# Loading K and V units in runs of 1 KB instead of 4 KB per partition

## The chip, the cores and the metric

The kernel runs on one core of one Trainium2 chip. The metric is the device time of one execution in microseconds. Every kernel was executed several times, and the tables give medians. The kernel before was run again beside each group of experiments, on the same chip. Its median was 697.37 us beside the change, and 700.1, 701.38 and 696.53 us beside the three groups of experiments. One of its runs beside the first group was marked as slow and is left out of the ratios.

## The reference

It is a decode step with two attention layers and two feed-forward layers that share their weights and their K and V caches:

```python
B, Sq, D = 4, 1, 512
Hq, Hkv, Sk, Dh = 32, 8, 8192, 128        # k_cache, v_cache: (B, Hkv, Sk, Dh), bf16, 67 MB each
...
scores = jnp.einsum("bhqd,bhkd->bhqk", q, k) * (Dh ** -0.5)
p = _softmax(scores, axis=-1)
o = jnp.einsum("bhqk,bhkd->bhqd", p, v)
...
x = x + _A_ref(_layernorm(x, axis=-1), A_k_cache, A_v_cache, A_wq, A_wo)   # attention
x = x + _B_ref(_layernorm(x, axis=-1), B_w_gate, B_w_up, B_w_down)         # feed-forward
x = x + _A_ref(...)                                                        # the same once more
x = x + _B_ref(...)
```

The softmax and the sum over keys do not depend on the order of the keys, as long as K and V are permuted alike.

## The kernel before

The caches are read in units of 2,048 rows of one head, 512 KB each. A unit goes into a slot with 4 KB in each of the 128 partitions. There are 7 ring slots, and 11 kept slots that hold some V units for the second layer. In all 468 units are loaded (256 of K, and 168 + 44 of V), all from the queue of the SP engine, in a fixed order. Each partition receives 16 neighbouring rows, one run of 4 KB:

```python
CR = 2048; NB = CR // P; NRING = 7; NRET = 11
ring = sb("ring", [P, NRING, NB * Dh], BF16)
kept = sb("kept", [P, NRET, NB * Dh], BF16)
# ... cut ...
def pump():                                  # issues loads in order while their slots are free
    while lptr[0] < len(loads):
        kind, x, sm = loads[lptr[0]]
        if kind == "w":
            T.dma("sp", x[0], x[1], sm, writes=[x[2]])       # a weight piece
        else:
            ap, key = home[x]
            if not released.get(key, True):
                return
            released[key] = False
            _, l, b, g, c = x
            cache = A_k_cache if x[0] == "k" else A_v_cache
            src = cache[b, g, c * CR:(c + 1) * CR, :].rearrange("(p t) d -> p (t d)", p=P)
            T.dma("sp", ap, src, sm, writes=[key])
        lptr[0] += 1
```

A K unit is transposed block by block on TensorE (16 transposes), copied out of PSUM by VectorE or ScalarE, and multiplied with q (4 matmuls). A V unit is the stationary operand of 16 matmuls with 4 columns:

```python
for t in range(8):                           # in k_front, for each half of a K unit
    blk = hf * 8 + t
    T.op("pe", lambda e: e.matmul(stg[:, t * P:(t + 1) * P], lhsT=ap[:, blk * Dh:(blk + 1) * Dh],
                                  rhs=ident[:], is_transpose=True, start=True, stop=True), ...)
# ... cut: in v_unit, for m in range(NM), j in range(NJ) ...
T.op("pe", lambda e: e.matmul(ps[:, bk * BW:bk * BW + REP],
                              lhsT=ap[:, (NM * j + m) * Dh:(NM * j + m + 1) * Dh],
                              rhs=pp[:, q, col:col + REP], ...), ...)
```

Between the streams of units lie stretches in which TensorE works on projections, feed-forward layers and softmax, and on kept V units that need no load in the second layer.

## Time and profile before

| | before |
|---|---|
| median time | 697.37 us |
| span of the profiled run | 699.7 us |
| TensorE (PE) busy | 584.9 us, 84% |
| share of the DMA engines in queue 1 | 96.1% |
| unit of 512 KB, from issue to landing | 7.6 us |

From the page of the profile of the kernel before (PE is TensorE, PEld its weight loads, DVE VectorE, ACT ScalarE; SPq is the SP engine's issuing queue): span and busy time; then, over 40 equal slices of the span, the granted TensorE clock in tenths, the busy share of the 16 DMA engines in tenths, and the GB/s that they moved; the packets by size; the queue of the loads with packets, MB and share of the engines; the chain of work that ended last; and the two costliest groups with "busy, mean ns of one | idle time before them, and what ended most of it".

```profile
span 699.7 us, 25539 instructions
...
PE 584.9 (84%) x11552; PEld 479.2 (68%) x11552; DVE 298.8 (43%) x635; ACT 235.1 (34%) x296; POOL 0.7 (0%) x6
...
PEclk9999879995589889985599879995589955599855
DMA  8999999999889999999999999999899989999992
GB/s 349 388 388 408 385 395 407 401 401 409 328 284 411 404 399 407 406 408 392 335 343 409 402 370 385 370 409 407 320 382 409 408 325 410 349 338 361 343 396 75
DMA packets 75117, 260.93 MB, mean 373 GB/s; under 512 B 7672, under 2 KB 13568, under 8 KB 74496
...
q1 hardware_dynamic: 75008, 259.30, 96.1%
...
PE 51%; DMA 37%; issue 5%; DVE 4%; ACT 2%; SPq 1%; ACTq 0%
DMA ring<-in_A_k_cache_dram 27%; PE ps L408 25%; PE ps L507 9%; DMA ring<-in_A_v_cache_dram 8%; PE ps L424 7%; PE ps L572 3%; PE ps L596 2%; DMA wq_sb<-in_A_wq_dram 2%; PE ps L531 1%; SPq L92 1%; PE ps L632 1%; PE ps L548 1%; ACT ktp L248 1%; PE ps L479 1%; DVE negm L436 1%
...
L408 PE MATMUL ps<-ident,ring 128*128 128x128 bf16 x4096 | 294.6, 230 | 36.8 <-DMA ring<-in_A_k_cache_dram 35.0
L408 PEld LDWEIGHTS ps<-ident,ring 128*128 128x128 bf16 x4096 | 251.4, 103 | 79.0 <-DMA ring<-in_A_k_cache_dram 54.1
...
ring<-in_A_k_cache_dram SPq DMA_DIRECT2D x256, 512.0 KB, 7.6
```

The reader should see three things here. The DMA engines are busy nearly throughout, at 385 to 411 GB/s in most slices. In some slices (328, 284, 335, 343, 320, 325 and so on) they move much less: there, TensorE is in a stretch that frees no ring slot. And the groups of TensorE on line 408, the K transposes, wait mostly for ring loads of K. The chain, with 37% DMA and 51% PE, passes between the two.

### The profile page before, as it was taken

What the parts mean: (1) busy time and instruction counts of PE and PEld (TensorE: products, weight loads), DVE (VectorE), ACT (ScalarE), POOL (GpSimd) and SP (SyncE); (2) the same over time, 40 slices, a digit from 0 to 9 for tenths busy, and PEclk for the clock granted to TensorE, in tenths of its full rate; (3) what the DMA queues carried; (4) which work ended last, traced back from release to release, by engine and by line L of the source; (5) the groups of instructions that cost most, each with busy time, mean ns of one, the idle gap of its engine ahead of it and who ended that gap; (6) DMA issues with size and microseconds to landing.
All of it is one profiled execution on the core that took longest, in us unless ns stands there. A gap on an engine that the chain in (4) does not pass through costs nothing.

```text
span 699.7 us, 25539 instructions
## 1 busy us (share of the span) xinstructions
PE 584.9 (84%) x11552; PEld 479.2 (68%) x11552; DVE 298.8 (43%) x635; ACT 235.1 (34%) x296; POOL 0.7 (0%) x6
## 2 busy tenths in 40 slices
PE   3977879878699899987799898988799876799876
PEld 2755657657677687766677677767777675777665
DVE  1544524443156645452165534543155510266501
ACT  1533324331056434420154434432055500055400
POOL 0000000000000000000000000000000000000000
PEclk9999879995589889985599879995589955599855
DMA  8999999999889999999999999999899989999992
GB/s 349 388 388 408 385 395 407 401 401 409 328 284 411 404 399 407 406 408 392 335 343 409 402 370 385 370 409 407 320 382 409 408 325 410 349 338 361 343 396 75
DMA packets 75117, 260.93 MB, mean 373 GB/s; under 512 B 7672, under 2 KB 13568, under 8 KB 74496
## 3 DMA queue, kind: packets, MB, share of 16 engines
q1 hardware_dynamic: 75008, 259.30, 96.1%
q8 instruction: 90, 1.47, 0.9%
q14 instruction: 19, 0.16, 0.1%
HBM read 259.26 MB, written 0.00 MB: 371 GB/s over the span
## 4 chain that ended last, share of the span: by engine, by line
PE 51%; DMA 37%; issue 5%; DVE 4%; ACT 2%; SPq 1%; ACTq 0%
DMA ring<-in_A_k_cache_dram 27%; PE ps L408 25%; PE ps L507 9%; DMA ring<-in_A_v_cache_dram 8%; PE ps L424 7%; PE ps L572 3%; PE ps L596 2%; DMA wq_sb<-in_A_wq_dram 2%; PE ps L531 1%; SPq L92 1%; PE ps L632 1%; PE ps L548 1%; ACT ktp L248 1%; PE ps L479 1%; DVE negm L436 1%
## 5 line engine op out<-in xcount | busy, mean ns | idle before, releaser
L408 PE MATMUL ps<-ident,ring 128*128 128x128 bf16 x4096 | 294.6, 230 | 36.8 <-DMA ring<-in_A_k_cache_dram 35.0
L408 PEld LDWEIGHTS ps<-ident,ring 128*128 128x128 bf16 x4096 | 251.4, 103 | 79.0 <-DMA ring<-in_A_k_cache_dram 54.1
L246 DVE COPY ktp<-ps 128x1024 bf16<-128x1024 bf16 x320 | 215.6, 689 | 206.3 <-PE ps L408 205.4
L248 ACT ACTIVATE ktp<-ps 128x1024 bf16<-128x1024 bf16 x192 | 195.5, 1023 | 259.7 <-PE ps L408 259.7
L424 PE MATMUL ps<-ktp,qpad 128*32 128x512 bf16 x1024 | 111.3, 401 | 3.3 <-ACT ktp L248 2.6
L507 PE MATMUL ps<-pp,ring 128*128 128x4 bf16 x2688 | 88.9, 166 | 22.5 <-issue 13.1
L507 PEld LDWEIGHTS ps<-pp,ring 128*128 128x128 bf16 x2688 | 82.5, 102 | 35.5 <-issue 21.8
L424 PEld LDWEIGHTS ps<-ktp,qpad 128*32 128x32 bf16 x1024 | 27.7, 93 | 37.7 <-ACT ktp L248 7.5
L507 PE MATMUL ps<-pp,kept 128*128 128x4 bf16 x1408 | 45.8, 166 | 8.7 <-DMA kept<-in_A_v_cache_dram 6.3
L507 PEld LDWEIGHTS ps<-pp,kept 128*128 128x128 bf16 x1408 | 41.4, 101 | 16.6 <-DMA kept<-in_A_v_cache_dram 7.9
L564 ACT ACTIVATE lnv<-var,eps_sb 128x4 f32<-128x4 f32 x10 | 3.0, 297 | 142.9 <-DVE var L551 142.9
L515 DVE TENSOR_TENSOR oT<-ps,invL 128x4 bf16<-128x4 f32 x64 | 10.6, 166 | 79.8 <-PE ps L507 79.7
L438 ACT ACTIVATE pp<-ps,negm 128x512 bf16<-128x512 f32 x32 | 22.0, 687 | 26.7 <-DVE negm L436 22.7
L572 PE MATMUL ps<-xnT,wq_sb 128*128 128x4 bf16 x640 | 18.7, 166 | 11.5 <-DMA wq_sb<-in_A_wq_dram 7.7
L436 DVE TENSOR_REDUCE negm<-ps 128x1 f32<-128x512 f32 x32 | 22.1, 690 | 11.6 <-PE ps L424 10.0
L572 PEld LDWEIGHTS ps<-xnT,wq_sb 128*128 128x128 bf16 x640 | 17.9, 104 | 12.0 <-DMA wq_sb<-in_A_wq_dram 7.8
L531 PE MATMUL ps<-oT,wo_sb 128*128 128x4 bf16 x640 | 21.3, 166 | 5.5 <-DVE oT L515 2.9
L531 PEld LDWEIGHTS ps<-oT,wo_sb 128*128 128x128 bf16 x640 | 20.0, 104 | 7.8 <-issue 4.7
L479 PE MATMUL ps<-ident,pp 128*128 128x128 bf16 x128 | 14.5, 303 | 1.3 <-DVE pp L469 1.0
L551 DVE TENSOR_REDUCE var<-ps 128x4 f32<-128x16 f32 x10 | 1.7, 175 | 28.2 <-PE ps L548 28.2
L479 PEld LDWEIGHTS ps<-ident,pp 128*128 128x128 bf16 x128 | 12.4, 140 | 1.9 <-DVE pp L469 1.7
L248 ACT ACTIVATE pp<-ps 128x1024 bf16<-128x1024 bf16 x6 | 6.1, 1025 | 16.8 <-PE ps L479 16.8
(66 smaller groups left out, 158.1 us busy)
## 6 DMA issues: line engine op xcount, KB each, us to landing
ring<-in_A_k_cache_dram SPq DMA_DIRECT2D x256, 512.0 KB, 7.6
ring<-in_A_v_cache_dram SPq DMA_DIRECT2D x168, 512.0 KB, 7.6
kept<-in_A_v_cache_dram SPq DMA_DIRECT2D x44, 512.0 KB, 12.2
wq_sb<-in_A_wq_dram SPq DMA_DIRECT2D x1, 4096.0 KB, 12.4
wo_sb<-in_A_wo_dram SPq DMA_DIRECT2D x4, 1024.0 KB, 11.6
wg_sb<-in_B_w_gate_dram SPq DMA_DIRECT2D x2, 896.0 KB, 12.0
wu_sb<-in_B_w_up_dram SPq DMA_DIRECT2D x2, 896.0 KB, 11.9
wd_sb<-in_B_w_down_dram SPq DMA_DIRECT2D x2, 896.0 KB, 9.2
```

What stands on the lines that cost most here:

```text
L246: T.op("dve", lambda e: e.tensor_copy(dst, src), reads=reads, writes=writes)
L248: T.op("act", lambda e: e.activation(dst, src, ACTF.Copy), reads=reads, writes=writes)
L408: T.op("pe", lambda e: e.matmul(stg[:, t * P:(t + 1) * P], lhsT=ap[:, blk * Dh:(blk + 1) * Dh], rhs=ident[:], is_transpose=True, start=Tru ...
L424: T.op("pe", lambda e: e.matmul(ps[32 * j:32 * (j + 1), bk * BW:(bk + 1) * BW], lhsT=qp, rhs=ktp[:, s, (j % 2) * 512:(j % 2 + 1) * 512], s ...
L436: T.op("dve", lambda e: e.tensor_reduce(negm[:, q, c:c + 1], bank(bk), AX.X, ALU.max, negate=True), reads=[f"pb{bk}"], writes=[f"negm{q}_{ ...
L438: T.op("act", lambda e: e.activation(pp[:, q, c * 512:(c + 1) * 512], bank(bk), ACTF.Exp, bias=negm[:, q, c:c + 1], scale=1.0, accum_out=l ...
L479: T.op("pe", lambda e: e.matmul(stg[:, t * P:(t + 1) * P], lhsT=pp[:, q, blk * P:(blk + 1) * P], rhs=ident[:], is_transpose=True, start=Tr ...
L507: T.op("pe", lambda e: e.matmul(ps[:, bk * BW:bk * BW + REP], lhsT=ap[:, (NM * j + m) * Dh:(NM * j + m + 1) * Dh], rhs=pp[:, q, col:col + ...
L515: T.op("dve", lambda e: e.tensor_tensor(oT[:, l, g * REP:(g + 1) * REP, b], ps[:, bk * BW:bk * BW + REP], invL[:, q, g * REP:(g + 1) * REP ...
L531: T.op("pe", lambda e: e.matmul(ps[:, OPJ * BW + nq * B:OPJ * BW + (nq + 1) * B], lhsT=wo_sb[:, h, nq * P:(nq + 1) * P], rhs=oT[:, l, h, : ...
L572: T.op("pe", lambda e: e.matmul(misc[:, h * B:(h + 1) * B], lhsT=wq_sb[:, kt, h * Dh:(h + 1) * Dh], rhs=xnT[:, kt * B:(kt + 1) * B], start ...
L596: T.op("pe", lambda e: e.matmul(ps[:, bk * BW + fo * B:bk * BW + (fo + 1) * B], lhsT=w_sb[:, kt, fo * P:(fo + 1) * P], rhs=xnT[:, kt * B:( ...
```

## The change

The intent is to read every K and V unit in smaller pieces: each partition holds four runs of four rows (1 KB) instead of one run of 16 rows. The four runs of a partition lie 128 KB apart in HBM. Bytes, number of DMAs, slots and all compute instructions stay.

```diff
     NRING = 7
+    NPIECE = 4
     NRET = 11
@@ in pump @@
-                    src = cache[b, g, c * CR:(c + 1) * CR, :].rearrange("(p t) d -> p (t d)", p=P)
-                    T.dma("sp", ap, src, sm, writes=[key])
+                    src = cache[b, g, c * CR:(c + 1) * CR, :].rearrange("(i p t) d -> p i (t d)", p=P, i=NPIECE)
+                    T.dma("sp", ap.rearrange("p (i x) -> p i x", i=NPIECE), src, sm, writes=[key])
```

Line numbers rise by one after it: line 408 of before is line 409 of after.

## The prediction

> What bounds it now. The DMA engines. The table of DMA queues gives queue 1 96.1% of the 16 engines' span; the slices show DMA at 9 tenths nearly throughout and about 405 GB/s where it is saturated. PE is busy 84% (busy table), but its largest idle groups wait for ring loads of K (54.1 and 35.0 us, groups table), and the chain of waits puts 37% on DMA. The queue is deep: a unit of 512 KB lands 7.6 us after issue, the time of six units at that rate. Only in a few slices (284, 320 to 340 GB/s) do the DMA engines wait, because PE works there on FFN, softmax and kept V units and frees no ring slot; I estimate about 40 us of such stalls, plus about 17 us without bulk loads at the start and the end (the FFN tail).
>
> What changes. 468 units of 512 KB (256 K, 168 + 44 V) are cut into 4 x 128 pieces of 1 KB: 59,904 packets of 4 KB become 239,616 of 1 KB. Bytes, DMA count, ring, and every instruction on PE, DVE, ACT and their order stay (the order listing shows only line numbers and the shape of the load change). Rows are permuted within a unit, in K and V alike, so the result holds.
>
> The cost. The before trace holds the same access form: the wo pieces are 128 partitions x 8 runs of 1 KB, with the same steps on the HBM side (1 KB between partitions, 128 KB between runs). Its packet records: a 4 KB packet has median 159 ns, mean 168; a 1 KB packet median 48, mean 50.3. Four small ones take 192 to 201 ns. In the stretches where only wo packets run (24.5 to 26.5 us, 33.5 to 34.5 us) the engines moved about 350 GB/s, against 405. The Trainium skill ("DMA: Bandwidth & Descriptors", Why small descriptors are slow) gives about 3 cycles per packet over 32-byte beats: 4 x 35 against 131 cycles, +7%. The trace shows more, +16 to +20%; I follow the trace.
>
> Sum, an estimate: units 245.4 MB / 350 GB/s = 701 us (now about 600); weights about 37; instruction fetches 6; start and tail 17: floor 761. Of the 40 us of stalls about half remain: slower loads partly fill the PE-only stretches, but the ring's seven units cannot cover long ones. Stretching every 10 us window of the trace to its new DMA demand where that is longer gives about 780. Nothing is removed; nearly all the added DMA time is on the critical path, since DMA was saturated and PE had the slack.
>
> Issue cost is not expected to bind: a unit takes 0.33 us of SP's queue now, a wo piece with twice the pieces of a new unit 0.43.
>
> Predicted: 781 us, 80% range 755 to 812. Faster by over 2%: 0.01; within 2%: 0.02; slower by over 2%: 0.97.
>
> What would show it. Right: about 240,000 1 KB packets, mean near 50 ns; saturated slices near 350 GB/s; queue 1 still at 95% or more; PE busy time about unchanged (585 us) at a share near 75%; longer waits of L409 (now L408) for ring loads of K; unit landing near 9 to 10 us. Wrong: DMA share clearly under 95% with SP solid in issues (descriptor generation binds); or slices still near 400 GB/s.
>
> What would make it wrong: 1 KB packets running slower than wo's when nothing else is mixed in (HBM access in steps, descriptor generation), giving 820 or more; or PE, granted a higher clock with more idle time, hiding the stalls wholly, giving about 760.

## More of the kernel before

From the waits of the DMA queue's own issuer in the kernel before (waiter, what it waited for, total us, times, longest):

```profile
SPq L62 <- PE ps L408: 263.9, 225, 11.8
SPq L62 <- PE ps L507: 157.9, 111, 8.3
```

SP stands for 422 us waiting for TensorE to free a slot. That does not make TensorE the limit: up to seven units may be under way while SP waits, and one unit needs 1.28 us at 409 GB/s, so much of this waiting can stand behind a full queue.

## The result, and the profile after

The change took 779.94 us at the median (777.56 to 780.51, 3 runs), against 697.37 us; the ratio of fast runs is 1.1175, with a 95% interval from 1.1141 to 1.1208. The predicted 781 us was 1 us off. The same lines of the page, of the kernel after:

```profile
span 775.8 us, 25539 instructions
...
PE 608.4 (78%) x11552; PEld 490.7 (63%) x11552; DVE 300.2 (39%) x635; ACT 235.5 (30%) x296; POOL 0.7 (0%) x6
...
PEclk9998768895599878995599958895589965589855
DMA  9999999999999999999999999999999999999992
GB/s 335 350 349 363 357 350 349 349 348 349 330 290 349 349 349 349 347 348 348 298 349 349 349 350 347 346 348 342 347 311 349 348 294 352 347 341 351 348 347 83
DMA packets 254829, 260.93 MB, mean 336 GB/s; under 512 B 7672, under 2 KB 253184, under 8 KB 254208
...
q1 hardware_dynamic: 254720, 259.30, 104.2%
...
PE 35%; DMA 30%; SPq 24%; issue 6%; DVE 3%; ACT 1%; ACTq 0%
SPq L92 24%; DMA ring<-in_A_k_cache_dram 20%; PE ps L409 18%; DMA ring<-in_A_v_cache_dram 7%; PE ps L508 6%; PE ps L425 5%; PE ps L573 2%; DMA wq_sb<-in_A_wq_dram 2%; DMA kept<-in_A_v_cache_dram 1%; PE ps L597 1%; PE ps L532 1%; PE ps L633 1%; ACT ktp L249 1%; DVE negm L437 1%; PE ps L549 1%
...
L409 PE MATMUL ps<-ident,ring 128*128 128x128 bf16 x4096 | 304.0, 234 | 63.6 <-DMA ring<-in_A_k_cache_dram 57.0
L409 PEld LDWEIGHTS ps<-ident,ring 128*128 128x128 bf16 x4096 | 259.6, 105 | 111.7 <-DMA ring<-in_A_k_cache_dram 91.0
...
ring<-in_A_k_cache_dram SPq DMA_DIRECT2D x256, 512.0 KB, 8.7
```

The same bytes come in 254,829 packets instead of 75,117. The GB/s row has become a flat line at 347 to 350, where its upper edge was at about 409, with many dents. A few dents remain (290, 298, 311, 294). The idle time ahead of the K transposes rose from 36.8 to 63.6 us on PE (35.0 and 57.0 us of it ended with a ring load of K) and from 79.0 to 111.7 us on the weight load (54.1 and 91.0 us).

The queue share of 104.2% means that packet records of one engine overlap a little. For that reason the rates below, and not the durations of single packets, are used for sums.

From the waits of the issuer in the kernel after:

```profile
SPq L62 <- PE ps L409: 91.4, 98, 5.2
SPq L62 <- PE ps L508: 73.2, 50, 6.0
```

SP's waiting for TensorE fell from 422 to 165 us. It now stands in the issues themselves: the median issue of a K unit took 1288 ns, where it took 328 ns before, and the chain puts 24% on "SPq L92". This line calls for a test, because it could mean that producing four times as many descriptors had become the limit.

### The profile page after: what moved, and what is told of

Its sections match the earlier page's. It is cut to its first block, busy times and chain, and to the rows that moved or that the text cites. A ratio compares the mean times of both kernels' runs of the same rounds, so it can differ in the third digit from the quotient of the medians.

```text
span 775.8 us, 25539 instructions
## 1 busy us (share of the span) xinstructions
PE 608.4 (78%) x11552; PEld 490.7 (63%) x11552; DVE 300.2 (39%) x635; ACT 235.5 (30%) x296; POOL 0.7 (0%) x6
## 2 busy tenths in 40 slices
DMA packets 254829, 260.93 MB, mean 336 GB/s; under 512 B 7672, under 2 KB 253184, under 8 KB 254208
## 3 DMA queue, kind: packets, MB, share of 16 engines
q1 hardware_dynamic: 254720, 259.30, 104.2%
## 4 chain that ended last, share of the span: by engine, by line
PE 35%; DMA 30%; SPq 24%; issue 6%; DVE 3%; ACT 1%; ACTq 0%
SPq L92 24%; DMA ring<-in_A_k_cache_dram 20%; PE ps L409 18%; DMA ring<-in_A_v_cache_dram 7%; PE ps L508 6%; PE ps L425 5%; PE ps L573 2%; DMA wq_sb<-in_A_wq_dram 2%; DMA kept<-in_A_v_cache_dram 1%; PE ps L597 1%; PE ps L532 1%; PE ps L633 1%; ACT ktp L249 1%; DVE negm L437 1%; PE ps L549 1%
## 5 line engine op out<-in xcount | busy, mean ns | idle before, releaser
L409 PE MATMUL ps<-ident,ring 128*128 128x128 bf16 x4096 | 304.0, 234 | 63.6 <-DMA ring<-in_A_k_cache_dram 57.0
L409 PEld LDWEIGHTS ps<-ident,ring 128*128 128x128 bf16 x4096 | 259.6, 105 | 111.7 <-DMA ring<-in_A_k_cache_dram 91.0
L508 PE MATMUL ps<-pp,ring 128*128 128x4 bf16 x2688 | 91.1, 166 | 40.4 <-DMA ring<-in_A_v_cache_dram 19.7
L425 PE MATMUL ps<-ktp,qpad 128*32 128x512 bf16 x1024 | 113.2, 412 | 3.3 <-ACT ktp L249 2.8
L508 PE MATMUL ps<-pp,kept 128*128 128x4 bf16 x1408 | 46.7, 166 | 14.0 <-DMA kept<-in_A_v_cache_dram 12.1
L587 DVE TENSOR_SCALAR qpad<-ps,qscale 128x16 bf16<-128x16 f32 (+1 forms) x12 | 2.9, 239 | 22.3 <-PE ps L573 22.1
```

The source lines that it names most:

```text
L425: T.op("pe", lambda e: e.matmul(ps[32 * j:32 * (j + 1), bk * BW:(bk + 1) * BW], lhsT=qp, rhs=ktp[:, s, (j % 2) * 512:(j % 2 + 1) * 512], s ...
L508: T.op("pe", lambda e: e.matmul(ps[:, bk * BW:bk * BW + REP], lhsT=ap[:, (NM * j + m) * Dh:(NM * j + m + 1) * Dh], rhs=pp[:, q, col:col + ...
```

## The experiments

Three theories stood against each other for the lower rate.

- Theory A: each packet costs a DMA engine a fixed time on top of its bytes.
- Theory B: the jumps in HBM cost, so where the runs lie matters and not their number.
- Theory C: the issuing side, which has to produce four times as many descriptors, is the limit.

A second question was how the higher cost of the stream reaches the total: the prediction claimed 101 us more stream, of which some 20 us would fill stretches in which the DMA engines had waited for TensorE.

The comparison with the reference is a weak guard: the kernel "compute_only" below attends stale cache rows and still passed it. That rows of K and V stay matched in the change rests on the code: K and V units are loaded by the same expression, and both are cut into blocks by position.

### p2k and p512: two and eight pieces

```diff
-    NPIECE = 4
+    NPIECE = 2        # p512: 8
```

> Two pieces of 2 KB instead of four of 1 KB. Theory A (a fixed cost per packet in the DMA engines; from the saturated rates of 405 GB/s at 4 KB and 349 at 1 KB an engine needs about 8.6 ns + 0.0374 ns per byte): a 2 KB packet needs about 85 ns, saturated slices near 385 GB/s, time about 722 us (+3 to +4.5%). Theory B (the 128 KB jumps in HBM between a partition's runs cost, whatever the piece size): half the jumps or, if any jump is bad, the full loss: 735 to 780 us and slices under 380 GB/s. Theory C (descriptor generation for the queue limits at about 341 packets per us): 2 KB packets would not be limited at all: about 697 us and 405 GB/s.

> Eight pieces of 512 B. Theory A: about 27.8 ns per packet, saturated slices near 295 GB/s, time about 885 to 905 us. Theory C (341 packets per us): 175 GB/s, over 1400 us. Theory B: at most as many bytes per second lost as jumps double: no firm number, but not the 295 GB/s of a line through 4 KB and 1 KB except by chance.

p2k took 723.3 us (ratio 1.0365, 1.0292 to 1.0438). p512 took 920.74 us (ratio 1.3198, 1.3113 to 1.3283). From the pages, p2k first, then p512:

```profile
GB/s 346 374 373 392 379 379 386 386 386 386 338 289 387 385 384 370 359 387 386 358 343 386 386 368 375 386 387 386 316 379 386 386 299 389 366 309 384 328 378 71
DMA packets 135021, 260.93 MB, mean 361 GB/s; under 512 B 7672, under 2 KB 13568, under 8 KB 134400
```

```profile
span 919.0 us, 25539 instructions
...
PE 665.2 (72%) x11552; PEld 529.7 (58%) x11552; DVE 301.4 (33%) x635; ACT 236.6 (26%) x296; POOL 0.7 (0%) x6
...
PEclk9888766765598777865588767775577865599855
...
GB/s 313 297 292 291 293 294 285 293 287 288 290 289 288 284 285 291 291 289 289 290 289 290 283 291 289 289 288 289 289 285 294 278 253 287 285 286 290 290 278 117
DMA packets 494445, 260.93 MB, mean 284 GB/s; under 512 B 7672, under 2 KB 492800, under 8 KB 493824
```

p2k hit Theory A's figure (722 us, 385 GB/s). Theory C falls with p512: a limit of 341 packets per us would have given 175 GB/s, and the slices show 283 to 297 apart from the two ends and three dents, half of them 288 to 291. The time of p512 missed the expected 885 to 905 us by 16 us; the line's two constants were slightly off and are taken afresh below from streams with nothing to compute beside them.

### near1k and far4k: where the runs lie

near1k keeps runs of 1 KB, but 2 KB apart instead of 128 KB. far4k keeps one run of 4 KB per partition, but neighbouring partitions read 16 KB apart.

```diff
 near1k, against the change
-  src = cache[b, g, c * CR:(c + 1) * CR, :].rearrange("(i p t) d -> p i (t d)", p=P, i=NPIECE)
+  src = cache[b, g, (c - c % 2) * CR:(c - c % 2 + 2) * CR, :].rearrange(
+            "(p i h t) d -> h p i (t d)", p=P, i=NPIECE, h=2)[c % 2]
 far4k, against the kernel before
-  src = cache[b, g, c * CR:(c + 1) * CR, :].rearrange("(p t) d -> p (t d)", p=P)
+  src = cache[b, g].rearrange("(p c t) d -> c p (t d)", p=P, c=NCH)[c]
```

> 1 KB pieces as in the change, but a partition's four runs lie 2 KB apart in an 8 KB stretch instead of 128 KB apart. Same number of packets and bytes. Theory A and C: as the change, 775 to 785 us, 349 GB/s. Theory B: back to about 697 to 715 us.

> 4 KB pieces as before, but neighbouring partitions read 16 KB apart (the four units of a group interleave in HBM) instead of back to back. Theory A and C: as before, 693 to 702 us. Theory B (scattered HBM reads cost): clearly slower, over 715 us.

near1k took 782.66 us (ratio 1.121, 1.1133 to 1.1287). From its page:

```profile
GB/s 337 348 348 363 357 348 348 348 348 348 316 270 348 348 348 348 346 348 348 315 330 349 349 349 348 344 349 348 315 330 349 349 278 346 348 311 348 348 347 92
DMA packets 254829, 260.93 MB, mean 334 GB/s; under 512 B 7672, under 2 KB 253184, under 8 KB 254208
```

far4k took 704.43 us (ratio 1.0089, 1.001 to 1.0168), 2 us above the expected range. From its page:

```profile
GB/s 352 381 386 408 375 389 409 408 406 408 308 300 410 393 380 387 352 409 407 355 339 409 400 364 358 409 399 407 312 378 409 407 322 411 368 345 366 333 384 62
```

Its saturated slices reach 406 to 411 GB/s. Runs of 1 KB cost the same whether they lie 128 KB or 2 KB apart, and whole runs of 4 KB in scattered places cost about 1% (0.1 to 1.7%). Theory B falls.

### wsplit1k: which side is cut

The source is one run of 4 KB per partition as before. Two slots share a stretch of the buffer in alternating runs of 1 KB, so that only the writing side is cut.

```diff
-  ring = sb("ring", [P, NRING, NB * Dh], BF16)
-  kept = sb("kept", [P, NRET, NB * Dh], BF16)
+  ring = sb("ring", [P, (NRING + NRET) // 2, 4, 2, NB * Dh // 4], BF16)
   # slot s is ring[:, s // 2, :, s % 2, :], kept slot s is slot NRING + s; the matmuls index it so
-  T.dma("sp", ap, src, sm, writes=[key])
+  T.dma("sp", ap, src.rearrange("p (i x) -> p i x", i=4), sm, writes=[key])
```

> Each partition reads one contiguous run of 4 KB, as before, but writes it as four runs of 1 KB (two units share a stretch of the buffer, interleaved). Theory A, with the packet cut by whichever side is shorter: as the change, 775 to 787 us, about 349 GB/s, packets of 1 KB in the records. Rival A2, the cost lies on the reading side alone: as before, 695 to 705 us.

It took 781.01 us (ratio 1.1198, 1.1145 to 1.125). From its page:

```profile
GB/s 336 349 349 364 353 349 348 348 348 347 322 266 349 348 350 348 346 348 348 296 344 347 348 348 343 346 349 348 337 346 348 349 274 352 345 289 349 348 348 84
DMA packets 254829, 260.93 MB, mean 334 GB/s; under 512 B 7672, under 2 KB 253184, under 8 KB 254208
```

The packet counts are those of the change to the last packet, although HBM is read in runs of 4 KB. The cost comes without any jump within a partition's run in HBM, which is the sharpest test against Theory B. In these runs a packet is as long as the shorter of the two contiguous runs, and it is the packet that costs. The records give one size per packet, so they cannot tell what each side pays by itself.

### after_v_on_act: two issuers

```diff
-  T.dma("sp", ap.rearrange("p (i x) -> p i x", i=NPIECE), src, sm, writes=[key])
+  T.dma("sp" if x[0] == "k" else "act", ap.rearrange("p (i x) -> p i x", i=NPIECE), src, sm, writes=[key])
```

> The change with the V units issued from ACT's queue, K and weights from SP's: two issuers generate descriptors. Theory A: the engines are the limit, slices stay at 349 GB/s or under, time 775 us or more (more if ACT is held up by issuing). Theory C (one issuer's descriptor generation limits): slices above 349 GB/s where K and V mix, clearly faster than 775 us.

It took 808.86 us (ratio 1.1529, 1.147 to 1.1587). From its page; then line 425 from the page of the change; then from the view of the issuing line of after_v_on_act (min/median/max ns of one issue):

```profile
GB/s 337 349 348 367 357 342 345 349 347 237 328 276 349 309 334 349 339 348 239 337 340 348 349 315 348 348 348 340 255 317 348 348 290 321 349 331 349 326 351 109
...
L425 PE MATMUL ps<-ktp,qpad 128*32 128x512 bf16 x1024 | 115.9, 413 | 42.0 <-ACT ktp L249 41.3
```

```profile
L425 PE MATMUL ps<-ktp,qpad 128*32 128x512 bf16 x1024 | 113.2, 412 | 3.3 <-ACT ktp L249 2.8
```

```profile
L92 SPq DMA_DIRECT2D ring<-in_A_k_cache_dram x256: 367/368/7378, 1.6 to 742.5; - x128
```

The median issue of a K unit is back at 368 ns (the shortest in the change took 367 ns too), so SP seldom stands in its issues, and yet no slice rises above 351 GB/s apart from two (367 and 357), which the change has too (363 and 357), at the place of the weights in longer runs. Together with p512 this refutes Theory C. So SP's 24% of the chain in the kernel after reads as a full queue: back pressure from the engines, and not what limits them. The run is slower than the change, with dents down to 237. The q matmuls of line 425 waited 41.3 us for ScalarE's copies, where they waited 2.8 us in the change: ScalarE was held up by its issues (the chain puts 9% on ACT's issuing queue). That this explains all of the 26 to 29 us is argued from these lines and was not tested further.

### stream4k, stream1k and compute_only: the two sides alone

The stream kernels issue every load in its order through the same slots, but consume each unit with one transpose and compute nothing else up to the last feed-forward layer; their results are wrong. compute_only computes everything, but loads each slot once only.

```diff
 stream4k and stream1k, in place of the phases
+  for u in order:
+      ap, key = home[u]
+      bk = next_bank()
+      T.op("pe", lambda e: e.matmul(bank_bf(bk)[:, 0:P], lhsT=ap[:, 0:P], rhs=ident[:],
+                                    is_transpose=True, start=True, stop=True),
+           reads=[key, "ident"], writes=[f"pb{bk}"])
+      release(u)
+      pump()
 compute_only
-  T.dma("sp", ap, src, sm, writes=[key])
+  if key not in filled:
+      filled.add(key)
+      T.dma("sp", ap, src, sm, writes=[key])
```

> The load stream of the kernel before alone: every DMA in its order through the same ring, but each unit is consumed by one transpose and nothing else is computed (except the last FFN); the result is wrong on purpose. From the before trace I estimate 606 us for the units at 405 GB/s, about 37 for weights, 6 for instruction fetches, some 17 for start and tail: 645 to 670 us, with no slice under 390 GB/s in the middle. If that holds, about 40 us of the 697 are stalls in which DMA waits for PE. If the stream alone takes over 685 us, there are no such stalls and that term of the prediction is wrong.

> The same with the change (1 KB pieces), wrong on purpose. Theory A: 100 us above the 4 KB stream, 745 to 770 us at 349 GB/s. The full change cost 82.6 us, so the difference of about 17 us would be stalls of before that the slower loads hide. If the stream costs only 83 us more, nothing was hidden.

> All computation, but each ring and kept slot is loaded only once, so PE waits for no unit after the start; wrong on purpose. PE is 585 us busy before: expected 610 to 670 us. If PE had the slack that the prediction claims, this is clearly under 697 and further under 780; if it takes 690 us or more, the kernel before was bound by PE as much as by DMA, and stalls could not be hidden by slower loads.

| kernel | median us | ratio to before (95% interval) |
|---|---|---|
| stream4k | 658.22 | 0.9396 (0.9351 to 0.9441) |
| stream1k | 762.97 | 1.0886 (1.0842 to 1.093) |
| compute_only | 601.82 | 0.8586 (0.8545 to 0.8627) |

From the pages of stream4k, stream1k and compute_only, in this order:

```profile
GB/s 346 392 387 404 408 390 409 411 409 410 410 409 410 409 410 409 410 410 409 411 408 410 409 410 410 409 410 409 410 410 410 408 287 407 410 410 409 409 410 101
...
q1 hardware_dynamic: 75008, 259.30, 99.8%
```

```profile
GB/s 334 348 348 362 362 348 348 348 348 348 348 348 348 348 348 348 348 348 348 348 348 348 348 348 348 348 347 349 348 348 348 337 292 348 348 348 348 348 348 123
...
q1 hardware_dynamic: 254720, 259.30, 107.1%
```

```profile
span 599.9 us, 24643 instructions
...
PE 559.0 (93%) x11552; PEld 463.3 (77%) x11552; DVE 298.0 (50%) x635; ACT 234.7 (39%) x296; POOL 0.7 (0%) x6
```

Both streams fell inside what was expected. They have one dent that was not forecast (287 and 292): in stream4k SP issued nothing from 531.3 to 538.6 us, because the next loads go to kept slots whose second-layer units were still to be consumed. compute_only came out 8 us under its range of 610 to 670 us; the slack on TensorE is a little larger than expected. The two sides alone need 658 and 602 us, and together 701.38 beside them. Of the difference to the stream (43 us), about 6 us are the instruction fetches that the full kernel has and the streams do not (the share of queue 8 is 0.9% of 699.7 us before and 0.0% in stream4k). The other 37 us or so are, by subtraction, stretches in which the stream waits for TensorE. The packet records of the kept traces bear this out: against stream4k the 16 engines of the kernel before lacked a packet for 22 us more (39.2 against 17.4 us, counted as packets under way short of 16, per engine), and its 4 KB packets took 18 us more per engine in sum (mean 168.2 against 163.4 ns), of which 6 us fall beside instruction fetches and nearly all the rest within 2 us of such a gap. The change makes the stream 0.149 of the kernel's time longer (1.0886 - 0.9396, 104.75 us of medians). The whole kernel pays 0.1175 (82.57 us of medians). The difference, 0.0315 or about 22 us (uncertain by some 3 us, as the two ratios are), was hidden in stretches in which the stream had waited before.

### The line of Theory A, with constants from the streams

The undisturbed slices of the streams are 410 GB/s at 4 KB and 348 at 1 KB. Sixteen engines then need 16 x 4096 / 410 = 159.8 ns and 16 x 1024 / 348 = 47.1 ns per packet. The line through both is 9.5 ns + 0.0367 ns per byte. Its forecasts for sizes that it was not made from:

| run length | line, ns per packet | line, GB/s | saturated slices |
|---|---|---|---|
| 512 B | 28.3 | 290 | mostly 288 to 291 (p512) |
| 1 KB | 47.1 | made from | 348 |
| 2 KB | 84.6 | 387 | 386 to 387 (p2k) |
| 4 KB | 159.8 | made from | 410 |
| 8 KB | 310.1 | 423 | 418 to 421 (pair8k, below) |

With 28.3 ns instead of 27.8 the expectation for p512 moves up by 479,232 packets x 0.5 ns / 16, or 15 us, to 900 to 920 us; the measured 920.74 us lies at its upper end.

A line through rates does not say whether the 9.5 ns are spent in each engine or in something that all 16 share. The packet records speak for the engine. In stream1k the 115 packets of 1 KB that ran with at most four under way took 46 ns at the median, and those with 14 to 18 under way took 51 ns; in stream4k packets of 4 KB took 159 ns (46 of them) and 162 ns. With most engines empty a packet is hardly shorter, so its time is the engine's own.

### pair4k and pair8k: the other direction

If packets cost 9.5 ns each, runs of 8 KB should help. Two neighbouring units then have to be loaded by one DMA into two neighbouring slots. That takes 8 ring and 10 kept slots (four more V loads) and an order in which pairs stay together. pair4k is the control with the same pairs in runs of 4 KB.

```diff
-  NRING = 7;  NRET = 11
+  NRING = 8;  NRET = 10        # and K units ordered in pairs of c, phases cut at pairs, weight loads placed anew
-  src = cache[b, g, c * CR:(c + 1) * CR, :].rearrange("(p t) d -> p (t d)", p=P)
-  T.dma("sp", ap, src, sm, writes=[key])
+  src = cache[b, g, c * CR:(c + 2) * CR, :].rearrange("(p h t) d -> p h (t d)", p=P, h=2)   # pair8k
+  src = cache[b, g, c * CR:(c + 2) * CR, :].rearrange("(h p t) d -> p h (t d)", p=P, h=2)   # pair4k
+  T.dma("sp", ap2, src, sm, writes=[key, key2])
```

> Control for the next: two neighbouring units loaded by one DMA of 1 MB into two neighbouring slots (8 ring and 10 kept slots, 4 extra V loads), in runs of 4 KB per partition. Bytes rise by 2.1 MB (5 us of stream) and slots come free in pairs: 697 to 720 us, saturated slices near 408 GB/s.

> The same with runs of 8 KB. Theory A (8.6 ns per packet and 0.0374 ns per byte): an 8 KB packet needs 315 ns, saturated slices near 416 GB/s, the stream 12 to 15 us shorter than in the control; part of it turns into stalls on PE, so 5 to 13 us below the control (1 to 2%). If only pieces under 4 KB cost anything, no difference. Against the kernel before: 685 to 710 us, so at best a small gain.

pair4k took 717.21 us (ratio 1.0278, 1.023 to 1.0325) and pair8k 714.68 us (ratio 1.0253, 1.021 to 1.0296). From the pages, pair4k first, then pair8k:

```profile
GB/s 351 387 387 408 381 397 380 375 411 408 324 308 389 376 399 390 380 410 371 351 365 405 403 356 368 360 409 381 327 350 396 403 316 408 373 360 379 352 380 74
...
q1 hardware_dynamic: 71808, 261.38, 95.4%
```

```profile
GB/s 355 395 397 413 403 406 400 361 421 415 259 380 411 359 383 359 362 418 359 338 371 385 385 367 368 363 390 418 340 368 393 402 312 421 362 357 356 380 369 70
...
q1 hardware_dynamic: 41600, 261.38, 94.1%
```

The saturated slices of pair8k do reach 418 to 421 GB/s, but the difference of 2.5 us between the two is smaller than expected (5 to 13 us) and their intervals overlap, so no gain is shown. The pairs alone cost 2.8%, which is more than the larger runs could return. pair8k also came out 5 us above the range given for it against the kernel before. The dents of pair8k are no fewer than those of its control (259, 340, 338 and 312 among others), and the DMA share is lower, 94.1 against 95.4%: its faster stream waits more. No version tried beats the kernel before.

## Why the prediction was right

**The bound.** It named the DMA engines and a slack on TensorE. The runs show 658 us for the stream alone and 602 us for the computation alone, so both parts hold.

**The rate at 1 KB.** The prediction took 350 GB/s from the weight pieces of the kernel before, which have the same form of access, and 405 GB/s for 4 KB. Measured were 348 and 410. It was right to read the price from records of the same trace. In the view of two windows of the kernel before in which nearly all packets are such pieces, the last number is the GB/s (before it: start and end, length, busy time and instructions of PE, PEld, DVE, ACT and POOL, the granted clock, the DMA share):

```profile
24.50:26.00 1.50, 1.50 (x27) 1.13 (x24) 1.35 (x3) 0.35 (x1) 0.00 (x0) 1.00 1.10 350
33.00:33.50 0.50, 0.50 (x11) 0.41 (x8) 0.33 (x1) 0.50 (x1) 0.00 (x0) 1.00 1.10 352
```

The windows that the prediction names (24.5 to 26.5 and 33.5 to 34.5 us) run on by half a microsecond into packets of 4 KB and give 368 and 367; its 350 is right for the pieces alone. The estimate from the Trainium skill, +7% (page "DMA: Bandwidth & Descriptors", section "Why small descriptors are slow", about 3 cycles per packet), would have given about 42 us for 4 x 35 against 131 cycles on a 600 us stream. It left out that section's second term, 32 bytes of descriptor metadata per operation; with one beat of 32 bytes more it is 4 x 36 against 132, +9%, an estimate of 55 us. The streams show 104.75 us.

**The sum.** The floor was put at 761 us with 6 us of instruction fetches, so at 755 without them; the stream alone, which has none, took 762.97. That term was 8 us short. The stalls before were put at 40 us, and about 37 were measured. About half of them were to remain, some 20 us; 37 less the 22 hidden ones leaves about 15. So the mechanism held term by term, but the 1 us is luckier than the terms: a stream that was 1% too short and stalls that were some 5 us too long partly cancelled, and the kernel before itself ran at 697.37 us beside the change and at 701.38 us beside the streams, a difference of about the same size.

**The issue cost** was rightly called not binding. Of the double sign that it gave for the opposite, one half, SP solid in issues, came in part (issues of 1288 ns) and meant only a full queue; the other half, a DMA share clearly under 95%, did not come (104.2%). The first half alone would have misled.

**PE.** Here a side statement was wrong: PE busy time was to stay at 585 us, and PE "granted a higher clock with more idle time" was named as a risk; what came is the opposite. PE busy rose to 608.4 us, and the granted clock of the profiled run fell from 0.811 to 0.787. In p512 it was 0.713 with 665.2 us for the same instructions. The rows of the granted clock above have more slices at 5 to 7 tenths in p512 than in the kernel before. The Trainium skill (page "TensorE: Matmul & The Clock Gate", section "Part 1: The HAM clock gate (the 'warmup' mystery)") says that the clock follows how busy TensorE was in recent windows and falls to half when idle. Traces agree: their clock records hold only the levels 1.0 and 0.5, and in the 3.4 us ahead of a step to 1.0 TensorE was busy for 96% of the time in the kernel before and 99% in the change, ahead of a step to 0.5 for 60% and 52% (means over the steps). The streams hold no clock record and test nothing here. What the lower clock cost in time was not tested; at 1 KB TensorE had slack.

Smaller signs: K units landed 8.7 us after issue (9 to 10 expected), PE's share was 78% (near 75% expected), the mean 1 KB packet took 51.1 ns (50 expected), and the queue's share was 104.2% (95% or more expected).

## What to carry to other kernels

Read the price of a new transfer shape from transfers of that shape that the trace already holds, as a rate over a stretch in which only they run; here this gave the stream to about 1%. Then ask how much of the stream's change the other engine hides: halving the runs from 4 to 2 KB cost 25 us of a calculated 36 (59,904 x 9.5 ns / 16), from 4 to 1 KB 82 of a measured 105, and from 1 KB to 512 B about 141 (1.3198 - 1.1175, of 700 us) of a calculated 142. The hidden part shrinks as the stream becomes the only limit. That it is nothing in the last step is not shown: no stream at 512 B was run, and some 15 us of stalls were left to fill. A long issue time on the issuing queue can be back pressure, as it was here; try a second issuer, or look for short issues of the same shape, before reading it as the limit.

## What the Trainium skill lacked or had wrong

- "DMA: Bandwidth & Descriptors", section "Why small descriptors are slow": about 3 cycles of overhead per packet and 32 bytes of descriptor metadata, together an estimate of 4.7 ns if these are four cycles of the page's 850 MHz. The runs from 512 B to 8 KB fit 9.5 ns per packet and engine. The slope of the same line, 0.0367 ns per byte, is 436 GB/s for 16 engines and agrees with the page's 435 GB/s ceiling (section "Where 436 GB/s comes from").
- The same page, section "Specifications": at least 512 B for line rate. At 512 B the slices show 290 GB/s, 71% of the 410 at 4 KB; 2 KB gives 386 and 1 KB 348.
- "Perfetto Trace Analysis", section "Contiguity and DMAs": contiguity only matters within an SBUF partition line. Read as a statement on the SBUF side alone, it fails here: in the change and in near1k each partition's line is one contiguous 4 KB and only the HBM side is cut, and they cost 11.8% and 12.1%; wsplit1k cuts only the SBUF side and costs 12.0%. The shorter run of either side counts.
- No page found says that a long issue on the SP queue shows a full queue: the median K issue took 1288 ns in the change and 368 ns with the V loads on another queue, with no gain in rate.
